# Four of seven low operand parts of the next token block computed ahead and fetched from DRAM; a small Sinkhorn product moved ahead in its slot

## The chip, the cores and the metric

The kernel runs on one core of a Trainium2 chip. The metric is the device time of one execution in microseconds (us); several timed runs are made and their median is given. A profiled execution, which leaves the trace, is made besides.

## The reference

Three stages follow one another, all in float32. Only the second and the third are touched by the change.

```python
def _attn_ref(q, k, v, tau): ...            # thresholded softmax attention, 4 x 8 x 576 x 64

def _moe_ref(x, w1, w2, w3, w_out):         # x: 2304 x 512
    a = x @ w1
    b = x @ w2
    h = a * b @ w3
    return (h @ w_out)

def _moe2_ref(x, w_gate, w1, w2):           # 8 experts
    logits = x @ w_gate
    P = np.exp(logits - logits.max())
    for _ in range(8):
        P /= P.sum(1, keepdims=True) + 1e-09
        P /= P.sum(0, keepdims=True) + 1e-09
        P *= N / E
    out = np.zeros((N, D))
    for e in range(E):
        h = np.maximum(x @ w1[e], 0.0)
        out += P[:, e:e + 1] * (h @ w2[e])
    return out
```

## The kernel before

Attention comes first and leaves x, transposed, in SBUF. In the shadow of the attention the product w3 @ w_out is formed, so that the first layer is `(a * b) @ w34`. From then on one class, `Moe`, does both layers in 120 **units**. A unit takes one piece of 256 hidden columns for one **token block** of 768 tokens. Units 0 to 23 are the first layer: three token blocks of eight units, in turn of kind "a" (x @ w1, kept in `ca`) and kind "b" (x @ w2, multiplied by `ca`). Units 24 to 119 are the eight experts, four units each, for each of the three token blocks. "Block 0" below is units 0 to 7, and a block change is unit 7 to 8, 15 to 16 or 23 to 24.

Each unit forms x @ w (512 deep, 2 x 2 halves) with seven products in place of eight, so it needs seven combinations of the four quarters of x and seven of w. `SLOTS` (line 505) lists the seven **slots**: which operand of x, which of w, which of the two PSUM banks px and py, and whether the slot adds to what is in the bank. Every float32 operand is split into a high part rounded to the matmul's format and a low part, the rest; a slot is six TensorE products (w high x high, w high x low, w low x high, for two halves of the depth), all at line 650. The seven operands of x lie in `xh[i]` and `xl[i]` and serve all units of a block, so at a block change they are made anew: three come straight from x, four from the sums `xs[0]` to `xs[3]`. `xsum` (line 631) makes a sum, on GpSimd (POOL) in slot 5 of the last four units of a block. `xsplit` makes one operand: the high part by a ScalarE copy (ACT, line 638) and the low part by a VectorE subtraction (DVE, line 639). An operand can only be overwritten when the last unit of the block before has used it.

The order of every engine's work is the order in which the code is written. For each slot the loop in `run` (line 857) issues the slot's six products (`mm1`), then `pop`, which sends a share of the second products (h @ w34 or h @ w2, line 720) of the unit before, then `evac`, which moves the slot's result out of PSUM with ACT and DVE, then xsplits, a step of the weight preparation of the next unit (`prep1`, on POOL and ACT), and loads and sums. `FIRST_SPLITS_AT` says after which slot each xsplit comes at a change in the first layer: operands of slots 0 and 1 after slots 4 and 6 of the last unit, those of slots 2 to 6 after slots 0 to 4 of the next unit. Names like u2, v, c, c2, hh and hl (lines 674 to 717) are the steps of `evac`; slots 5 and 6 both use py, so slot 6 can only start when DVE has taken slot 5's result.

Weights of the first layer are prepared in block 0 alone. `keep` (line 555) writes them to DRAM from units 0 to 7, and `prep1` (line 580) reads them back in blocks 1 and 2; the copy out of a buffer must land before the buffer is loaded again. All DMAs are issued by SyncE (SP), in order, on one queue.

After the gate products (line 799) of the last token block, in unit 25, the eight Sinkhorn rounds run as a generator, `sinkhorn`, one small step per slot in units 25 to 30. Each round has one TensorE product of a matrix of ones with the column sums (line 833), which goes to spare columns of px or py; DVE reads the result at line 834.

Of the kernel before, what the change touches and what calls it, by code (L numbers as in the profile page):

```python
# [9 lines left out]
F32 = mybir.dt.float32  # L10
F32R = mybir.dt.float32r
AF = mybir.ActivationFunctionType
ALU = mybir.AluOpType
# [12 lines left out]
HT = SB // 2  # L26
# [2 lines left out]

SPLITS_AT = ((0, 0), (1, 1), (2, 2), (3, 3), (8, 4), (9, 5), (10, 6))  # L30

FIRST_SPLITS_AT = ((4, 0), (6, 1), (7, 2), (8, 3), (9, 4), (10, 5), (11, 6))

CONVERT = (0, 0, 1, 1, 1, 2, 0, 1, 3, 2, 0, 1, 1, 1, 2, 2, 1, 1)
PRODUCTS = (1, 0, 0, 0, 4, 1, 1, 0, 4, 1, 0, 0, 2, 4, 2, 3, 3, 4)
# [28 lines left out]
def f32(ap):  # L64
    return ap.bitcast(F32)
# [434 lines left out]
class Moe:  # L500
# [126 lines left out]
    def xsum(self, s, i, eng):  # L627
# [2 lines left out]
                      (b(0, 1), self.xs[1], ALU.subtract), (b(0, 0), b(1, 0), ALU.subtract))[i]  # L630
        eng.tensor_tensor(out=self.xs[i], in0=x0, in1=x1, op=op)

    def xsplit(self, s, slot):

        i = self.SLOTS[slot][0]
        src = {0: lambda: self.xblock(s, 0, 0), 1: lambda: self.xblock(s, 0, 1), 2: lambda: self.xblock(s, 1, 1),
               3: lambda: self.xs[0], 4: lambda: self.xs[1], 5: lambda: self.xs[3], 6: lambda: self.xs[2]}[i]()
        self.nc.scalar.activation(self.xh[i], src, AF.Copy)  # L638
        self.nc.vector.tensor_tensor(out=self.xl[i], in0=src, in1=f32(self.xh[i]), op=ALU.subtract)  # L639

# [201 lines left out]
    def run(self):  # L842
        units = self.units
        self.raw1[0] = self.k.raw0
        prep = self.prep1(0)
        for slot in range(7):
            if slot < 4:
                self.xsum(0, slot, self.nc.vector)
            self.xsplit(0, slot)
            if slot >= 1:  # L850
                next(prep, None)
            yield
        for _ in prep:
            pass
        sink = None
        gates = {8 * s + (12 if s + 1 < NSB else 9): s for s in range(NSB)}
        for u, (kind, s, j) in enumerate(units):
            nxt = units[u + 1] if u + 1 < len(units) else None
            while u == 1 and self.pool2 is None:
                yield  # L860
            if kind != "a":
                self.hs[u] = tuple(self.pool2.tile([128, 2, SB], F32R, tag=t, name=f"{t}{u}", bufs=2)
                                   for t in ("hh", "hl"))
            ahead = [units[min(u + i, len(units) - 1)][1] for i in range(5)]
            splits = {}
            if ahead[1] != s:
                splits = dict(FIRST_SPLITS_AT if kind == "b" else SPLITS_AT)
            elif u and units[u - 1][1] != s:
                splits = {at - 7: slot for at, slot in (FIRST_SPLITS_AT if units[u - 1][0] == "b" else SPLITS_AT)}
            prep = self.prep1(u + 1)  # L870
            self.load1(u + 2)
            for slot in range(7):
                yield
                late, self.late = self.late[:2], self.late[2:]
                self.mm1(u, slot)
                gate = self.gate(gates[u], slot) if u in gates and slot in (2, 4, 6) else None
                self.pop(slot)
                if sink:
                    try:
                        sink.send(self.xy[1 if slot < 4 else 0])  # L880
                    except StopIteration:
                        sink = None
                self.evac(u, slot)
                if gate:
                    gate()
                    if u == 8 * NSB + 1 and slot == 6:
                        sink = self.sinkhorn()
                        next(sink)
                for f in late:
                    f()  # L890
                if slot in splits:
                    self.xsplit(ahead[1], splits[slot])
                next(prep, None)
                if u < 8 and slot in (1, 2):
                    self.keep(u, slot - 1)
                if slot == 5 and ahead[4] != s:
                    self.xsum(ahead[4], next(i for i in range(4) if ahead[3 - i] == s), self.nc.gpsimd)
                if slot in (3, 5):
                    self.prep2(u + 1 if kind == "a" else u, (slot - 3) // 2)
            while self.later:  # L900
                self.later.pop(0)()
            if kind == "b":
                self.queue_b(u)
                self.left = (2 if nxt[0] == "a" else 1) * (6 + SHARE)
            elif kind != "a":
                self.queue_d(u)
                self.left = 6 + SHARE
        self.left = 0
        self.pop(6)
        for f in self.late:  # L910
            f()
# [3 lines left out]
def kernel(ctx, tc, qk, vv, tau, w1, w2, w3, wo, wg, e1, e2, out):  # L915
    k = Ctx()
# [9 lines left out]
    k.w64 = {"a": w1, "b": w2}  # L926
    k.w34 = dram.tile([4, 128, 2, DM], F32, name="w34")
    k.wab = {n: dram.tile([4, 128, 1024], F32, name=f"w_{n}") for n in ("a", "b")}
    k.wk = dram.tile([8, 2, 128, 7 * 256], F32, name="w_kept")
    k.moe = None  # L930
    attention(k)
# [43 lines left out]
```

## Time and profile before

| | |
|---|---|
| timed runs | 2241.58, 2244.11, 2244.15 us; median 2244.11 |
| profiled execution | 2245.75 us; span of its instructions 2243.8 us |
| granted TensorE clock, mean | 0.996 |
| busy, share of the span | TensorE 97%, VectorE 54%, ScalarE 42%, GpSimd 45% |

The span is the time from the first to the last instruction of the profiled execution; the execution takes 1.95 us more. PE is TensorE, DVE VectorE, ACT ScalarE, POOL GpSimd and SP SyncE. A matmul's shown time overlaps that of its neighbours: two neighbouring 384-column products start 0.17 us apart though each is shown with 0.33 us. An arrow in brackets behind a row gives the idle time of the engine before the instruction and what ended it.

### The profile page before, as it was taken

Reading aid. Unit: us, or ns where it says so; the run is one execution under the profiler, and the core shown is the slowest. Engines: PE = TensorE matmul, PEld = TensorE weight load, DVE = VectorE, ACT = ScalarE, POOL = GpSimd, SP = SyncE. Lnnn points to the kernel's source line nnn. Section 1 sums busy time; section 2 is a strip of 40 time slices with the busy share of each in tenths; the row PEclk is TensorE's granted clock in tenths of the full one; section 3 lists DMA queues with packets and bytes.
Section 4 is the critical chain, followed back from the end, with each engine's and each line's share of the span. In section 5 each row is a group of like instructions: output and inputs, shape, how many; then the busy total and the mean of one; then the engine's idle time right before and its main releaser. Section 6 shows DMA issues by size and latency. Waiting matters only on the chain.

```text
span 2243.8 us, 32239 instructions
## 1 busy us (share of the span) xinstructions
PE 2177.2 (97%) x12624; PEld 1895.7 (84%) x12624; DVE 1222.2 (54%) x2110; ACT 938.4 (42%) x1758; POOL 1013.6 (45%) x982
## 2 busy tenths in 40 slices
PE   7899999899999999999999999999999999999999
PEld 4666666698988888999999999999999999999997
DVE  6888888655455565444445544444445534444443
ACT  6877777532132333333334333333334343333332
POOL 4545444671012444444446544444446444444441
PEclk9999999999999999999999999999999999999999
DMA  4343434455443112122121221212212222121121
GB/s 136 101 129 117 124 107 128 153 205 220 151 182 114 57 57 76 57 76 72 60 75 57 104 75 57 76 58 75 76 57 76 88 72 75 57 76 64 69 75 38
DMA packets 59352, 208.67 MB, mean 93 GB/s; under 512 B 7104, under 2 KB 11200, under 8 KB 59200
## 3 DMA queue, kind: packets, MB, share of 16 engines
q1 hardware_dynamic: 59200, 206.61, 26.6%
q8 instruction: 99, 1.62, 0.3%
q14 instruction: 53, 0.43, 0.1%
HBM read 180.90 MB, written 25.69 MB: 92 GB/s over the span
## 4 chain that ended last, share of the span: by engine, by line
PE 70%; DVE 1%; issue 0%; ACT 0%; POOL 0%; DVEq 0%; ACTq 0%
PE ye L720 36%; PE py L650 19%; PE px L650 14%; DVE xl L639 0%; PE py L799 0%; DVE c L694 0%; PE px L799 0%; DVE c L705 0%; DVE prob L837 0%; ACT xh L638 0%; DVE acc L774 0%; POOL w1l L594 0%; DVE hl L716 0%; POOL w1l L591 0%; DVE small L834 0%
## 5 line engine op out<-in xcount | busy, mean ns | idle before, releaser
L720 PE MATMUL ye<-w2h,hl 128*128 128x512 f32 x1152 | 451.3, 392 | 0.0
L720 PE MATMUL ye<-w2h,hh 128*128 128x512 f32 x1152 | 451.1, 392 | 0.0
L720 PE MATMUL ye<-w2l,hh 128*128 128x512 f32 x1152 | 450.8, 391 | 0.0
L715 ACT ACTIVATE hh<-c 128x384 fp32r<-128x384 f32 x288 | 151.5, 526 | 610.4 <-DVE c L694 610.3
L596 POOL TENSOR_TENSOR w1l<-wt,w1h 128x1024 fp32r<-128x1024 f32 x104 | 252.6, 2429 | 286.2 <-ACT w1h L593 286.2
L650 PE MATMUL py<-xh,w1h 128*128 128x384 f32 x960 | 323.3, 337 | 7.6 <-DVE c L694 3.6
L650 PE MATMUL py<-xl,w1h 128*128 128x384 f32 x960 | 323.1, 337 | 3.5 <-DVE xl L639 3.5
L650 PE MATMUL py<-xh,w1l 128*128 128x384 f32 x960 | 322.7, 336 | 0.3 <-POOL w1l L596 0.3
L591 POOL TENSOR_TENSOR w1l<-raw,w1h 128x256 fp32r<-128x256 f32 x104 | 79.2, 762 | 479.5 <-ACT w1h L585 479.5
L650 PE MATMUL px<-xh,w1h 128*128 128x384 f32 x720 | 243.4, 338 | 4.7 <-ACT p L674 1.6
L650 PE MATMUL px<-xl,w1h 128*128 128x384 f32 x720 | 242.7, 337 | 2.7 <-DVE xl L639 2.7
L720 PEld LDWEIGHTS ye<-w2l,hh 128*128 128x128 f32 x1152 | 216.3, 188 | 32.6
L720 PEld LDWEIGHTS ye<-w2h,hl 128*128 128x128 f32 x1152 | 216.2, 188 | 32.6
L650 PE MATMUL px<-xh,w1l 128*128 128x384 f32 x720 | 242.1, 336 | 0.0
L720 PEld LDWEIGHTS ye<-w2h,hh 128*128 128x128 f32 x1152 | 216.3, 188 | 24.6
L650 PEld LDWEIGHTS py<-xh,w1h 128*128 128x128 f32 x960 | 180.6, 188 | 31.2 <-DVE c L694 6.0
L650 PEld LDWEIGHTS py<-xl,w1h 128*128 128x128 f32 x960 | 180.5, 188 | 22.3 <-DVE xl L639 5.3
L677 DVE TENSOR_TENSOR u<-py,p 128x384 f32<-128x384 f32 x120 | 66.7, 556 | 215.8 <-PE py L650 214.9
L650 PEld LDWEIGHTS py<-xh,w1l 128*128 128x128 f32 x960 | 180.4, 188 | 0.7 <-POOL w1l L596 0.7
L584 POOL TENSOR_TENSOR wt<-raw 128x512 f32<-128x512 f32 x104 | 139.7, 1343 | 77.8 <-DMA raw<-in_e 61.0
L716 DVE SCALAR_TENSOR_TENSOR hl<-c,hh 128x384 fp32r<-128x384 f32 x288 | 165.2, 573 | 9.2
L715 ACT ACTIVATE hh<-px 128x384 fp32r<-128x384 f32 x96 | 47.2, 492 | 272.9 <-PE px L650 272.9
(135 smaller groups left out, 3907.5 us busy)
## 6 DMA issues: line engine op xcount, KB each, us to landing
raw<-in_e SPq DMA_DIRECT2D x192, 512.0 KB, 4.0
wraw<-in_w SPq DMA_DIRECT2D x32, 512.0 KB, 4.1
w1h<-w_kept SPq DMA_DIRECT2D x16, 896.0 KB, 5.2
w1l<-w_kept SPq DMA_DIRECT2D x16, 896.0 KB, 7.0
rq<-in_qk SPq DMA_DIRECT2D x30, 288.0 KB, 5.3
w_kept<-w1h SPq DMA_DIRECT2D x8, 896.0 KB, 7.5
w_kept<-w1l SPq DMA_DIRECT2D x8, 896.0 KB, 9.1
raw<-w SPq DMA_DIRECT2D x12, 512.0 KB, 3.7
```

Of the source, the lines that this page charges most:

```text
L584: nc.gpsimd.tensor_tensor(out=t[:, 0:2], in0=raw[:, 1:3], in1=raw[:, 0:2], op=ALU.subtract)
L591: nc.gpsimd.tensor_tensor(out=wl[:, 0], in0=raw[:, 0], in1=f32(wh[:, 0]), op=ALU.subtract)
L596: nc.gpsimd.tensor_tensor(out=wl[:, 3:7], in0=t, in1=f32(wh[:, 3:7]), op=ALU.subtract)
L650: self.nc.tensor.matmul(out, lhsT=w[:, wi, o], rhs=x[xi][:, d], start=n == 0 and not adds, stop=n == 5, skip_group_check=True)
L677: tt(out=self.u2, in0=py, in1=self.p1, op=ALU.add)
L715: nc.scalar.activation(hi, src, AF.Relu)
L716: self.later.append(lambda: nc.vector.scalar_tensor_tensor(out=lo, in0=src, scalar=0.0, in1=f32(hi), op0=ALU.max, op1=ALU.subtract))
L720: self.queue.append((out.shape[-1], lambda: self.nc.tensor.matmul(out, lhsT=l, rhs=r, start=start, stop=stop, skip_group_check=True)))
```

## The change

Four things change.

1. For the operands of slots 0 to 3 at each of the three block changes of the first layer, the low parts are computed ahead. `xstage` makes the high part (ACT) and the low part (DVE) in the still unused accumulator `acc`, and SP stores the low part in a DRAM tensor `x_low`. It runs after slot 3 of the block's unit 2, slots 1 and 5 of unit 4 and slot 2 of unit 6 (`STAGED`).
2. At the change, `xturn` replaces `xsplit` for these four: ACT writes the high part again and SP loads the low part, after slots 1 to 4 of the block's last unit, one slot after the operand's last use. The other three operands are split as before, after slots 1 to 3 of the next unit.
3. The sums `xs` for these three changes are made on DVE, after slots 0 and 5 of unit 2 and slots 0 and 3 of unit 4 (`XSUMS`), instead of on POOL. The copies of unit 7's weights to DRAM go from slots 1 and 2 to slots 4 and 5.
4. The Sinkhorn step of a slot is issued before `pop` instead of behind it, and its ones product goes to px after slots 2, 4 and 5 and to py after the others (before: py up to slot 3, px from slot 4 on).

The block changes of the second layer keep their order.

```diff
-FIRST_SPLITS_AT = ((4, 0), (6, 1), (7, 2), (8, 3), (9, 4), (10, 5), (11, 6))
+XSUMS = {2: (0, 5), 4: (0, 3)}
+STAGED = {2: ((3, 0),), 4: ((1, 1), (5, 2)), 6: ((2, 3),)}
+NEXT_SB = (1, 2, 0)
...
+    def xstage(self, r, slot, n):
+
+        src = self.xsource(NEXT_SB[r], self.SLOTS[slot][0])
+        flat = self.acc.rearrange("p a b -> p (a b)")
+        hi, lo = (flat[:, 2 * HT * (2 * n + m):2 * HT * (2 * n + m + 1)].bitcast(F32R) for m in range(2))
+        split = lambda t: t.rearrange("p (a b) -> p a b", a=2)
+        self.nc.scalar.activation(split(hi), src, AF.Copy)
+        self.nc.vector.tensor_tensor(out=split(lo), in0=src, in1=split(f32(hi)), op=ALU.subtract)
+        self.nc.sync.dma_start(self.k.xk[r, slot], f32(lo))
+
+    def xturn(self, r, slot):
+
+        i = self.SLOTS[slot][0]
+        self.nc.scalar.activation(self.xh[i], self.xsource(NEXT_SB[r], i), AF.Copy)
+        self.nc.sync.dma_start(f32(self.xl[i]).rearrange("p a b -> p (a b)"), self.k.xk[r, slot])
...
-            splits = {}
-            if ahead[1] != s:
-                splits = dict(FIRST_SPLITS_AT if kind == "b" else SPLITS_AT)
+            splits, turns = {}, {}
+            if kind == "b" and ahead[1] != s:
+                turns = {i + 1: i for i in range(4)}
+            elif u and units[u - 1][0] == "b" and units[u - 1][1] != s:
+                splits = {i - 3: i for i in range(4, 7)}
+            elif ahead[1] != s:
+                splits = dict(SPLITS_AT)
             elif u and units[u - 1][1] != s:
-                splits = {at - 7: slot for at, slot in (FIRST_SPLITS_AT if units[u - 1][0] == "b" else SPLITS_AT)}
+                splits = {at - 7: slot for at, slot in SPLITS_AT}
...
-                self.pop(slot)
                 if sink:
                     try:
-                        sink.send(self.xy[1 if slot < 4 else 0])
+                        sink.send(self.xy[0 if slot in (2, 4, 5) else 1])
                     except StopIteration:
                         sink = None
+                self.pop(slot)
                 self.evac(u, slot)
...
-                if u < 8 and slot in (1, 2):
-                    self.keep(u, slot - 1)
-                if slot == 5 and ahead[4] != s:
+                at = 4 if u == 7 else 1
+                if u < 8 and slot in (at, at + 1):
+                    self.keep(u, slot - at)
+                if slot in turns:
+                    self.xturn(u // 8 if kind == "b" else u // 8 - 1, turns[slot])
+                if kind in ("a", "b"):
+                    if slot in XSUMS.get(u % 8, ()):
+                        self.xsum(NEXT_SB[u // 8], u % 8 - 2 + XSUMS[u % 8].index(slot), self.nc.vector)
+                    for at, x in STAGED.get(u % 8, ()):
+                        if slot == at:
+                            self.xstage(u // 8, x, at // 3 % 2)
+                elif slot == 5 and ahead[4] != s:
                     self.xsum(ahead[4], next(i for i in range(4) if ahead[3 - i] == s), self.nc.gpsimd)
...
+    k.xk = dram.tile([3, 7, 128, 2 * HT], F32, name="x_low")
```

The order of the instructions shows where this moves work. First DVE at the first block change, from the last results of unit 7 to slot 6 of unit 8. In the names the number behind u2, v, c, c2, hh and hl is the unit (and the next one the slot), the number behind xl and xh the operand, and the last number only tells tiles apart. Before:

```order
L694 TENSOR_TENSOR c_7_4_6038<-px_5189,v_7_3_6027 128x384
L639 TENSOR_TENSOR xl0_5117<-x_63,xh0_5110 128x768
L694 TENSOR_TENSOR c_7_5_6053<-py_5190,v_7_3_6027 128x384
...
L639 TENSOR_TENSOR xl4_5121<-s1_5125,xh4_5114 128x768
L705 TENSOR_TENSOR c2_7_6_6069<-c_7_6_6067,ca_5228 128x384
...
L639 TENSOR_TENSOR xl1_5118<-x_63,xh1_5111 128x768
L677 TENSOR_TENSOR u2_8_1_6109<-py_5190,p1_8_0_6090 128x384
L639 TENSOR_TENSOR xl3_5120<-s0_5124,xh3_5113 128x768
L639 TENSOR_TENSOR xl6_5123<-s2_5126,xh6_5116 128x768
L680 TENSOR_TENSOR v_8_3_6138<-py_5190,u2_8_1_6109 128x384
L639 TENSOR_TENSOR xl5_5122<-s3_5127,xh5_5115 128x768
```

The changed kernel, the same place:

```order
L726 TENSOR_TENSOR c2_7_6_6088<-c_7_6_6086,ca_5229 128x384
L728 TENSOR_TENSOR hl7_5995<-c2_7_5_6074,hh7_5994 128x384
L728 TENSOR_TENSOR hl7_5995<-c2_7_6_6088,hh7_5994 128x384
L698 TENSOR_TENSOR u2_8_1_6124<-py_5191,p1_8_0_6107 128x384
L660 TENSOR_TENSOR xl6_5124<-s2_5127,xh6_5117 128x768
L660 TENSOR_TENSOR xl5_5123<-s3_5128,xh5_5116 128x768
L701 TENSOR_TENSOR v_8_3_6153<-py_5191,u2_8_1_6124 128x384
L660 TENSOR_TENSOR xl2_5120<-x_63,xh2_5113 128x768
```

Four of the seven subtractions into xl are gone from here; xl6, xl5 and xl2 now stand nearer to the start of unit 8.

Second, SP's queue from the same unit 7 on, in the changed kernel (w_kept are the weights kept in DRAM, raw2 the weights of the second products; the number behind w1h and w1l is the unit):

```order
L608 DMA raw2_11_5983<-w34_64 128x1024
L582 DMA w1h8_6006<-w_kept_68 128x1792
L582 DMA w1l8_6007<-w_kept_68 128x1792
L653 DMA xl0_5118<-x_low_67 128x768
L653 DMA xl4_5122<-x_low_67 128x768
L653 DMA xl1_5119<-x_low_67 128x768
L557 DMA w_kept_68<-w1h7_5900 128x1792
L653 DMA xl3_5121<-x_low_67 128x768
L557 DMA w_kept_68<-w1l7_5901 128x1792
L582 DMA w1h9_6109<-w_kept_68 128x1792
L582 DMA w1l9_6110<-w_kept_68 128x1792
```

Before, the same rows stood there in the same order without the four loads of xl. The loads are new, and each waits for the slot that last used its buffer.

Third, DVE in unit 2 of the changed kernel, from the end of unit 1's work to the end of unit 2's (ca is where an a unit's results go):

```order
L728 TENSOR_TENSOR hl1_5361<-c2_1_6_5446,hh1_5360 128x384
L633 TENSOR_TENSOR s0_5125<-x_63 128x768
L698 TENSOR_TENSOR u2_2_1_5486<-py_5191,p1_2_0_5467 128x384
L701 TENSOR_TENSOR v_2_3_5517<-py_5191,u2_2_1_5486 128x384
L646 TENSOR_TENSOR acc_5341<-x_63,acc_5341 128x768
L711 TENSOR_TENSOR ca_5229<-px_5190,v_2_3_5517 128x384
L711 TENSOR_TENSOR ca_5229<-py_5191,v_2_3_5517 128x384
L633 TENSOR_TENSOR s1_5126<-s0_5125,x_63 128x768
L621 TENSOR_TENSOR w2l3_5552<-raw2_3_5344,w2h3_5524 128x1024
L711 TENSOR_TENSOR ca_5229<-py_5191,u2_2_1_5486 128x384
```

The rows at lines 633 (two sums) and 646 (the staged low part) are new here; the rest stands as before.

## Rows read from the trace of the kernel before

**Rows 1.** The page: busy time of the engines; a group of POOL's weight preparation.
```profile
PE 2177.2 (97%) x12624; PEld 1895.7 (84%) x12624; DVE 1222.2 (54%) x2110; ACT 938.4 (42%) x1758; POOL 1013.6 (45%) x982
...
L584 POOL TENSOR_TENSOR wt<-raw 128x512 f32<-128x512 f32 x104 | 139.7, 1343 | 77.8 <-DMA raw<-in_e 61.0
```

**Rows 2.** PE's timeline (start us, duration us, instruction): first products of units, two waits.
```profile
469.20 0.44 PE L650 MATMUL px<-xh,w1h 128*128 128x384 f32 x1 [0.15 <-ACT p L674]
...
493.85 0.44 PE L650 MATMUL px<-xh,w1h 128*128 128x384 f32 x1 [1.44 <-ACT p L674]
...
502.69 0.34 PE L650 MATMUL px<-xh,w1h 128*128 128x384 f32 x1
...
513.65 0.34 PE L650 MATMUL px<-xh,w1h 128*128 128x384 f32 x1
...
531.22 0.33 PE L650 MATMUL px<-xh,w1h 128*128 128x384 f32 x1
...
542.17 0.34 PE L650 MATMUL px<-xh,w1h 128*128 128x384 f32 x1
...
554.16 0.34 PE L650 MATMUL px<-xh,w1h 128*128 128x384 f32 x1
...
761.03 0.33 PE L650 MATMUL px<-xh,w1h 128*128 128x384 f32 x1
...
846.08 0.34 PE L650 MATMUL px<-xh,w1h 128*128 128x384 f32 x1
...
861.63 0.34 PE L650 MATMUL px<-xh,w1h 128*128 128x384 f32 x1
```

**Rows 3.** Busy us: PE, PEld, DVE, ACT, POOL; clock, DMA share, GB/s; PE's longest wait.
```profile
515.00:531.00 16.00, 12.32 (x67) 10.20 (x67) 13.35 (x16) 6.71 (x10) 9.24 (x4) 1.00 0.34 114
716.00:739.00 23.00, 19.43 (x103) 16.51 (x102) 19.35 (x24) 10.62 (x17) 16.50 (x11) 1.00 0.00 1
...
PE py L650 <- DVE xl L639: 1.1, 2, 0.6
```

**Rows 4.** By line: durations ns min/median/max, first and last start us.
```profile
L639 DVE TENSOR_TENSOR xl<-s,xh x24: 921/959/2125, 411.7 to 1739.3; 128x768 fp32r<-128x768 f32 x24
...
L638 ACT ACTIVATE xh<-s x24: 827/836/849, 410.8 to 1738.4; 128x768 fp32r<-128x768 f32 x24
```

**Rows 5.** Timelines of DVE and of POOL around 487 us, in unit 5.
```profile
486.76 0.56 DVE L694 TENSOR_TENSOR c<-py,v 128x384 f32<-128x384 f32 x1 [0.94 <-PE py L650]
487.23 2.04 DVE L705 TENSOR_TENSOR c<-c,ca 128x384 f32<-128x384 f32 x1
...
484.40 2.65 POOL L596 TENSOR_TENSOR w1l<-wt,w1h 128x1024 fp32r<-128x1024 f32 x1 [2.26 <-ACT w1h L593]
487.01 1.85 POOL L631 TENSOR_TENSOR s<-s,x 128x768 f32<-128x768 f32 x1
```

**Rows 6.** PE's timeline at one of the eight ones products.
```profile
804.24 0.39 PE L720 MATMUL ye<-w2l,hh 128*128 128x512 f32 x1
804.47 0.28 PE L833 MATMUL py<-small,ones 128*128 128x8 f32 x2
805.67 0.44 PE L650 MATMUL px<-xh,w1h 128*128 128x384 f32 x1 [0.92 <-DVE hl L716]
```

**Rows 7.** DMA in 502:517 (packets, MB, share; issue, landing us); SP's timeline; a stretch.
```profile
q1 hardware_dynamic: 795, 4.73, 92.9%
...
w_kept<-w1l SPq DMA_DIRECT2D x1, 896.0 KB, 11.8
...
513.50 0.32 SPq L580 DMA_DIRECT2D w1h<-w_kept  x1
515.78 0.32 SPq L580 DMA_DIRECT2D w1l<-w_kept  x1
...
534.00:536.00 2.00, 2.00 (x12) 1.87 (x11) 1.10 (x2) 0.00 (x0) 0.00 (x0) 1.00 1.06 428
```

**Rows 8.** The stretches' view again, 444:446.
```profile
444.00:446.00 2.00, 1.87 (x8) 1.58 (x8) 1.88 (x4) 1.50 (x4) 0.21 (x1) 0.50 0.83 221
```

More of the change, by code (lines that the diff above doesn't have):

```diff
@@ L631, in xsum, with xsource @@
         eng.tensor_tensor(out=self.xs[i], in0=x0, in1=x1, op=op)
+    def xsource(self, s, i):
+        return {0: lambda: self.xblock(s, 0, 0), 1: lambda: self.xblock(s, 0, 1), 2: lambda: self.xblock(s, 1, 1),
+               3: lambda: self.xs[0], 4: lambda: self.xs[1], 5: lambda: self.xs[3], 6: lambda: self.xs[2]}[i]()
+    def xstage(self, r, slot, n):
[10 more added lines that the diff above has]
+        self.nc.sync.dma_start(f32(self.xl[i]).rearrange("p a b -> p (a b)"), self.k.xk[r, slot])
     def xsplit(self, s, slot):
         i = self.SLOTS[slot][0]
-        src = {0: lambda: self.xblock(s, 0, 0), 1: lambda: self.xblock(s, 0, 1), 2: lambda: self.xblock(s, 1, 1),
-               3: lambda: self.xs[0], 4: lambda: self.xs[1], 5: lambda: self.xs[3], 6: lambda: self.xs[2]}[i]()
+        src = self.xsource(s, i)
         self.nc.scalar.activation(self.xh[i], src, AF.Copy)
```

## The prediction

> **What bounds the kernel now.** I read the page first. TensorE (PE) is busy 97% of the span [rows 1], so time can only come out of the few stretches in which PE stands still or runs slowly; everything on other engines counts only where PE waits for it. Next I read PE's timeline for the start of each unit: 42 L650 products a unit, seven slots of six, always beginning with px<-xh,w1h. The reader should see how even the starts are where nothing waits: 542.17 to 554.16 is 11.99 us for an a unit, 502.69 to 513.65 is 10.96 us for a b unit, 846.08 to 861.63 is 15.55 us for a unit of the second layer [rows 2]. Excess over these lengths is what a stall really costs, more than the idle time shown, because the product after a stall also starts the pipe again.
>
> Four places have excess. (1) Unit 8, the first of token block 1: 513.65 to 531.22 is 17.57 us, 5.58 too long. (2) Unit 16 repeats it a block later, 5.51 too long (its rows read like those of unit 8, the second of two such places). (3) Units 23 and 24: no unit of like length stands beside 24, so I go by idle time: PE is idle 3.57 us in 716:739 against 3.68 in 515:531 [rows 3], and 5.58 x 3.57 / 3.68 = 5.4. (4) Units 26 to 30, the Sinkhorn: 761.03 to 846.08 is 85.05 us, five units of 15.55 are 77.75, so 7.30; eight pairs of ones products at 0.28 [rows 6] are 2.24 of it and stay, 5.06 is waiting. A fifth is small: unit 6 waits 1.44 us at 493.85 [rows 2].
>
> Who is waited for? In 515:531 the longest waits of PE are for DVE's xl split [rows 3]. The split is seven ACT copies (0.84 us) and seven DVE subtractions of 0.96 us that stretch to 2.1 us [rows 4]. Why they stretch is seen best at 487: POOL starts a sum of 1.85 us at 487.01, and DVE's c<-c,ca, which reads only SBUF, takes 2.04 us and ends 0.41 us after POOL, while c<-py,v of the same size, with an operand in PSUM, had run in 0.56 us under another POOL instruction [rows 5]. I read this as exclusion: a DVE instruction that reads only SBUF and one of POOL wait for each other whole.
>
> **The change, part by part.**
>
> *Block changes (units 7/8, 15/16, 23/24).* Four of the seven DVE subtractions leave each change and become a DMA; three stay, one in each of slots 1 to 3 of the next unit. Working through unit 8 from its start at 513.65 with slots of 1.63 us (1.04 and five short L720 products): DVE loses xl0, xl4, xl1 and xl3 (4 x 0.96) ahead of u2 and v, POOL's sums no longer run beside it, and the other three, each behind its ACT copy (0.84), end about 4.6, 6.8 and 8.2 us in, while slots 4, 5 and 6 want them 6.7, 8.3 and 10.5 us in. ACT's copies start four slots earlier; the last ends before slot 5. So I take all 16.5 us (5.58 + 5.51 + 5.4) and give back what is late next. That is the DMA queue in unit 7: SP issues raw2, two kept loads, xl0, xl4, xl1, a copy out, xl3, a copy out, then unit 9's loads. The queue is already 92.9% busy in 502:517 [rows 7]; 4 x 384 KB = 1.57 MB add 3.7 us at the 428 GB/s of 534:536 and 4.6 us at the 339 that 4.73 MB in 92.9% of 15 us make. Unit 9's loads were issued at 513.50 and 515.78, when the copies out of the same buffers had landed; now the second goes out about 3.9 us later, at 519.6, landing near 525.5 to 527, while unit 9 would start at 525.6. I take 0.4 us (bounds 0 and 1.4). In units 23 and 24 POOL still prepares weights, so xl5 and xl2 meet it: 0.3 (bounds 0 and 1.5). Unit 16 has no copies out: 0.1. Sum -15.7. If instead every load took the 11.8 us of the slowest row, xl0 (issued at 503.8) would be 1.8 us late and unit 9 about 3 us; 3 us at each of three changes leave -7.5, the worst end.
>
> The Trainium skill ("DMA: Bandwidth & Descriptors", Specifications) puts a core's HBM limit at about 358 GB/s; the 428 of rows 7 lies above it, so the trace disagrees. By the page the four loads would take 4.4 us and unit 9 would wait 1.1 us instead of 0.4, 0.7 us more in all.
>
> *Staging in units 2, 4, 6 and 10 to 22.* Each block gets four sums on DVE (the size of xl, so 0.96 us where POOL is quiet), four ACT copies (0.84) and four subtractions (0.96) [rows 4]. In blocks 1 and 2 POOL has nothing to do, and an a unit leaves DVE over 1 us free in most slots: nothing, except units 12 and 20, where the gate products write py right behind slot 2 and u2, one sum later, is not yet out of it: 0.15 each, 0.3. Block 0 is different: POOL prepares weights in every slot, and the eight added instructions read SBUF only. Unit 2, from the end of slot 5's products: copy out of py 0.56, s1 0.96, w2l 1.2, next copy out 0.56, 3.3 us in all. PE wants the bank again, in unit 3's slot 1, after 3.9 us: eight L720 products of 0.23 [rows 6] and two slots of 1.04 (a b unit is 42 and 16 products: (10.96 - 16 x 0.23) / 7). So 0.6 us are spare, and s1 and w2l, each meeting a POOL weight instruction of up to 1.34 us (L584 [rows 1]) half way through, take 1.4: 0.8 late. Unit 4 has the same chain with a subtraction in the sum's place (0.5, since PE has been held once already) and, before it, s3 behind POOL's longest instruction, 2.65 us [rows 5], of which some 1.7 are left and the slots' slack covers half: 0.9, together 1.4. Against that, POOL's sum at 487.01 goes; what stays is what unit 4 shows at the same place, where POOL has only weights: an idle of 0.15 us at 469.20 against 1.44 at 493.85 [rows 2], 1.3 gained. Block 0 nets +0.9. Bounds: -1.6 (both idles gone, no new wait) and +2.9 (units 2 and 4 each as bad as unit 6 was).
>
> SP's twelve stores and the later raw loads behind them: raw1_7 leaves some 2.5 us later and lands about 1 us before POOL wants it; nothing. The moved copy-out of unit 7 is in the queue sum above.
>
> *Sinkhorn.* The ones product moves ahead of the slot's four to eight L720 products. At 804.47 it is the last of its slot; on DVE hl<-px stands behind the reading of its result, and PE's next slot waits 0.92 us for hl [rows 6]. Sent first, it is done about 1.15 us (five L720 products of 0.23) earlier, more than the 0.92. All eight places have at least four such products, 0.92 us. The bank choice keeps the next slot's bank free in all but one case, which has 1.15 us to spare. New danger: PE now waits if DVE's column sums are not ready at the end of the slot; only in unit 27 are they close. Of 5.06 I take 4.1 (bounds 0 and 5.1).
>
> **Sum.** -15.7 + 0.9 + 0.3 - 4.1 = -18.6 us. The profiled execution took 2245.75 us, which gives 2227.2; it lies 1.64 above the median of the three timed runs (2244.11), so for the median 2225.5. I forecast **2225.5 us**.
>
> **The rivals.** *The wait moves into block 0:* the eight added DVE instructions meet POOL harder than I count, units 2 to 6 each lose what unit 6 lost. For: POOL prepares weights there in every unit. Against: a units have slack. Five units by 1.44 are 7.2 in place of 0.9: 2231.8.
>
> *The low parts land late:* the loads take the slowest row's time, block changes give 7.5 instead of 15.7: 2233.7. For: 92.9% of the queue is taken. Against: only unit 7 has copies out beside them.
>
> *Slower:* the new stalls of units 2 and 3 stand right behind a stretch at a granted clock of 0.50, the 1.2 GHz level (444:446 [rows 8]): 8 matmuls in 2 us, against 12 at full clock in 534:536 [rows 7]. If they bring that level back, a unit of 12 us takes half as long again, 6 us more. From (18.6 + 4.5) / 6 = 3.9 units on, the kernel is slower by over 0.2%; five units give 2225.5 + 30 = 2255.5. Against: 3.68 us of idle in 515:531 left the clock at 1.00 [rows 3]. The Trainium skill ("TensorE: Matmul & The Clock Gate", Part 1) calls the low level the default and says that activity lifts it; by that rule a change that takes idle out of PE can hardly lower it, and no run here shows otherwise.
>
> *The relief does nothing:* ACT, which still makes all seven copies in order, becomes what is waited for; 5 us a change come back, 2242. Against: ACT was busy 6.71 of the 16 us of 515:531 [rows 3].
>
> **How the numbers follow.** Forecast 0.63, block 0 0.13, late loads 0.14, no relief 0.06, slower 0.04. About 0.2% (4.5 us) is the least that a measurement of this kernel tells from no change. The first three are faster: 0.90; no relief counts as the same: 0.06; slower 0.04. Low end: 2244.1 - 16.5 - 1.6 - 5.1 = 2220.9, so 2220.5. High end: late loads with a Sinkhorn that gives 2 less, 2235.7, so 2236.
>
> **What would show it.** Right: units 8 and 16 last under 12.6 us, no PE wait on xl or xh at 515 to 531; unit 9 starts within 0.5 us; units 26 to 30 sum to about 81 us; DVE subtractions in units 2 and 4 of 1.5 to 3 us beside POOL. Wrong: PE waits for an xl DMA in units 8, 16 or 24, units 2 to 5 above 13.5 us, granted clock under 1 after 446 us, or ones products followed by waits as long as now.

## The result and the profile after

| | before | after |
|---|---|---|
| timed runs, us (median; from, to; five each) | 2244.11; 2241.39, 2244.31 | 2220.82; 2218.66, 2223.54 |
| ratio, 95% interval | | 0.9903 [0.9889, 0.9916] |
| span of the profiled execution, us | 2243.8 | 2221.6 |
| from the start of unit 3 to the end of the last matmul, us | 1783.70 | 1763.05 |

The change makes the kernel 1.0% faster. The forecast was 2225.5 us, the range 2220.5 to 2236. The direction was right, and so was the mechanism of the two large terms; the forecast was 4.7 us too cautious, and the result lies just above the low end. The last row of the table is the sharpest measure. Ahead of unit 3 executions of one program differ: unit 3 began at 450.2 to 454.7 us in the thirteen profiles of this study. From unit 31 to the last matmul all thirteen took between 1392.2 and 1392.3 us. So below I compare units with units.

The page of the changed kernel, busy time of the engines, answers to [rows 1]:

```profile
PE 2171.8 (98%) x12624; PEld 1894.7 (85%) x12624; DVE 1229.4 (55%) x2122; ACT 947.1 (43%) x1770; POOL 990.9 (45%) x970
```

PE has the same number of matmuls; twelve instructions are gone from POOL, and DVE and ACT have twelve more each. POOL lost 22.7 us of busy time for twelve sums. DVE gained only 7.2 us, where twelve more instructions of 0.96 us are 11.5 us: some of its busy time before was stretching.

PE's timeline of the changed kernel (start us, duration us, instruction, in brackets the idle before it and what ended it), first products of units 7, 8, 9, 26 and 31, beside [rows 2]:

```profile
502.55 0.34 PE L671 MATMUL px<-xh,w1h 128*128 128x384 f32 x1
...
513.51 0.34 PE L671 MATMUL px<-xh,w1h 128*128 128x384 f32 x1
...
525.49 0.34 PE L671 MATMUL px<-xh,w1h 128*128 128x384 f32 x1
...
744.64 0.33 PE L671 MATMUL px<-xh,w1h 128*128 128x384 f32 x1
...
825.47 0.34 PE L671 MATMUL px<-xh,w1h 128*128 128x384 f32 x1
```

Unit 8 lasts 11.98 us, what an a unit takes with no wait, instead of 17.57. Units 26 to 30 last 80.83 in place of 85.05. The stretches (busy us and count of PE, PEld, DVE, ACT, POOL; clock, DMA share, GB/s) around units 8 and 24, where [rows 3] had 3.68 and 3.57 us of PE idle:

```profile
508.00:524.00 16.00, 16.00 (x97) 15.26 (x96) 10.89 (x19) 7.71 (x12) 0.00 (x0) 1.00 0.97 345
...
708.00:724.00 16.00, 16.00 (x94) 14.96 (x93) 14.35 (x20) 8.23 (x14) 11.50 (x9) 1.00 0.01 2
```

In these two stretches PE does not stand still at all. All waits of PE from 504 to 828 us (engine, line, released by: us in total, times, longest):

```profile
PE px L854 <- DVE small L851: 0.4, 1, 0.4
```

One is left, the ones product of unit 27, which the forecast named as the new danger. It costs more than the 0.4 us shown: unit 27 lasts 17.24 us, 1.2 more than units 29 and 30, which have as many ones products and last 16.00 and 16.02. By line, DVE's subtractions: the three that stayed at the block change (500 to 530 us), and the staged ones from x in units 2 and 4 (durations in ns, min/median/max):

```profile
L660 DVE TENSOR_TENSOR xl<-s,xh x2: 959/959/959, 517.0 to 519.3; 128x768 fp32r<-128x768 f32 x2
L660 DVE TENSOR_TENSOR xl<-x,xh x1: 950/950/950, 520.6 to 520.6; 128x768 fp32r<-128x768 f32 x1
...
L646 DVE TENSOR_TENSOR acc<-x,acc x2: 2089/2324/2559, 449.4 to 476.2; 128x768 fp32r<-128x768 f32 x2
```

Against [rows 4]: the stretched subtractions are gone from the block change and stand in block 0 instead, 2.6 us in unit 2 and 2.1 us in unit 4, beside POOL's weight work. Only the one in unit 4 costs PE anything that a run shows (block 0 at slot 6, below).

### The profile page after: what moved, and what is told of

Read it like the earlier page. It is cut to its first block, busy times and chain, and to the rows that moved or that the text cites. A ratio compares the mean times of both kernels' runs of the same rounds, so it can differ in the third digit from the quotient of the medians.

```text
span 2221.6 us, 32300 instructions
## 1 busy us (share of the span) xinstructions
PE 2171.8 (98%) x12624; PEld 1894.7 (85%) x12624; DVE 1229.4 (55%) x2122; ACT 947.1 (43%) x1770; POOL 990.9 (45%) x970
## 4 chain that ended last, share of the span: by engine, by line
PE 92%; DVE 6%; issue 1%; ACT 1%; DMA 1%; POOL 0%; SPq 0%; ACTq 0%; DVEq 0%; POOLq 0%
PE ye L741 40%; PE py L671 22%; PE px L671 16%; PE s L142 4%; PE pv L232 3%; PE t L186 2%; PE w L460 2%; DVE p L161 2%; DVE nmx L146 2%; PE vs L209 1%; PE tt L197 1%; PE py L820 0%; DVE x L281 0%; DVE cvq L495 0%; DVE c L726 0%
## 5 line engine op out<-in xcount | busy, mean ns | idle before, releaser
L741 PE MATMUL ye<-w2h,hl 128*128 128x512 f32 x1152 | 451.6, 392 | 0.0
L741 PE MATMUL ye<-w2h,hh 128*128 128x512 f32 x1152 | 451.3, 392 | 0.0
L741 PE MATMUL ye<-w2l,hh 128*128 128x512 f32 x1152 | 451.0, 391 | 0.0
L741 PEld LDWEIGHTS ye<-w2l,hh 128*128 128x128 f32 x1152 | 216.3, 188 | 32.9 <-DVE w2l L621 0.3
L741 PEld LDWEIGHTS ye<-w2h,hl 128*128 128x128 f32 x1152 | 216.2, 188 | 32.6
L741 PEld LDWEIGHTS ye<-w2h,hh 128*128 128x128 f32 x1152 | 216.3, 188 | 24.6
```

The costliest lines, as they stand in the source:

```text
L741: self.queue.append((out.shape[-1], lambda: self.nc.tensor.matmul(out, lhsT=l, rhs=r, start=start, stop=stop, skip_group_check=True)))
```

## The experiments

Two theories stood behind the forecast's largest term: DVE's queue of seven in-order subtractions, and POOL's sums that shut DVE out. The experiments take them apart, put a price on the DMA queue and on the Sinkhorn's two edits, and look at what the forecast had missed. Lengths of units in us, one profile each (the two profiles of before and of the change in one column where they agree within 0.05):

| | before | change | sums only | staging only | ones late | copies early | loads beside |
|---|---|---|---|---|---|---|---|
| unit 5 | 10.96 | 11.96, 11.36 | 10.96 | 11.50 | 11.96 | 11.36 | 11.36 |
| unit 6 | 13.72 | 12.43 | 12.41 | 13.70 | 12.43 | 12.40 | 12.41 |
| unit 7 | 10.96 | 10.96 | 10.96 | 12.79 | 10.96 | 10.97 | 10.96 |
| unit 8 | 17.57 | 11.98 | 15.08 | 13.52 | 11.98 | 14.69 | 15.57 |
| unit 16 | 17.50 | 11.98 | 15.06 | 12.00 | 11.98 | 11.97 | 11.98 |
| units 23, 24 | 32.01 | 26.62 | 31.55 | 27.41 | 26.62 | 26.62 | 26.62 |
| units 26 to 30 | 85.05 | 80.83, 81.10 | 81.24 | 80.88 | 85.38 | 81.20 | 80.73 |

**Sums only.** Nothing is staged, the sums stay on DVE:

```diff
-STAGED = {2: ((3, 0),), 4: ((1, 1), (5, 2)), 6: ((2, 3),)}
+STAGED = {}
+FIRST_SPLITS_AT = ((4, 0), (6, 1), (7, 2), (8, 3), (9, 4), (10, 5), (11, 6))
...
-                turns = {i + 1: i for i in range(4)}
+                splits = dict(FIRST_SPLITS_AT)
...
-                splits = {i - 3: i for i in range(4, 7)}
+                splits = {at - 7: slot for at, slot in FIRST_SPLITS_AT}
```

> The sums stay on VectorE and ahead, but nothing is staged: all seven subtractions go back to the block change, in the slots they had. My theory (VectorE's own queue of in-order subtractions in front of PE's u2 and v copies is the larger part of the loss, POOL's sums beside them the smaller): unit 8 and unit 16 last 14 to 15.5 us, each with about 3 us of PE waits, unit 5 falls from 11.96 to about 11.0 because its staged pair is gone; time 2228 to 2230 us. Rival (POOL's sums, which lock VectorE out, are the whole cause, and moving the sums alone would have done): units 8 and 16 last 12.0 to 12.5 us, time 2220 to 2222 us.

2231.7 us, ratio to before 0.9947 [0.9932, 0.9962]. By line, DVE's subtractions of this kernel from 500 to 530 us, and PE's waits from 508 to 524:

```profile
L661 DVE TENSOR_TENSOR xl<-s,xh x4: 949/954/959, 511.0 to 518.9; 128x768 fp32r<-128x768 f32 x4
L661 DVE TENSOR_TENSOR xl<-x,xh x3: 948/951/959, 505.7 to 520.3; 128x768 fp32r<-128x768 f32 x3
```
```profile
PE px L672 <- DVE xl L661: 0.5, 1, 0.5
PE py L672 <- DVE xl L661: 0.5, 1, 0.5
PE px L672 <- ACT xh L660: 0.4, 1, 0.4
PE py L672 <- ACT xh L660: 0.3, 1, 0.3
```

With POOL idle no subtraction is stretched any more, and yet unit 8 keeps 3.10 of its 5.59 us. So the queue of splits alone costs 3.1 us, and POOL's sums beside it had added 2.5. At the third change, where POOL has weights to prepare anyway, taking its sums away gives only 0.5 of 5.4 us. I had named units 8 and 16 alone, and the time came out 1.7 us above the top of what I expected. Part of the 3.10 is ACT: its copies, in the old places, are late too (0.7 us of the 1.7 us of waits), so the change's earlier copies matter beside the staged low parts. No run moved the copies alone, so how the 3.10 divide between copies and subtractions is not shown.

**Staging only.** The staging stays, the sums go back to POOL. Since POOL makes the sum for slot 1's operand only in unit 5, that operand's staging moves from unit 4 to slot 5 of unit 6:

```diff
-XSUMS = {2: (0, 5), 4: (0, 3)}
-STAGED = {2: ((3, 0),), 4: ((1, 1), (5, 2)), 6: ((2, 3),)}
+STAGED = {2: ((3, 0),), 4: ((5, 2),), 6: ((2, 3), (5, 1))}
...
-                    if slot in XSUMS.get(u % 8, ()):
-                        self.xsum(NEXT_SB[u // 8], u % 8 - 2 + XSUMS[u % 8].index(slot), self.nc.vector)
+                    if slot == 5 and u % 8 > 3:
+                        self.xsum(NEXT_SB[u // 8], u % 8 - 4, self.nc.gpsimd)
```

> The other half alone: four low parts are staged as in the change, but the sums go back to POOL in slot 5 of units 4 to 7 of each block. Theory (three subtractions are few enough, and POOL's last sum is over before they begin): units 8 and 16 last 12.0 to 12.5 us; unit 6 gets its wait back, 13.4 to 13.8 us against 12.43, unit 5 loses its own, 11.0 to 11.4; time 2220.5 to 2223 us. Rival (the sums must leave POOL, staging is not enough): units 8 and 16 last 13.5 us or more, time 2225 us or above.

2224.35 us, ratio 0.9914 [0.9899, 0.9929]. In unit 16 the theory holds to 0.02 us, though a sum of POOL's still stretches one of its three subtractions to 1.85 us: three have room for it, seven had not. So the staging, with its earlier copies, is what that block change needed, and POOL's sums cost there only while the long queue stood. At the third change 0.8 us of 5.4 are lost. In block 0 the theory does not hold: units 7 and 8 lose 1.83 and 1.54 us, and the time is 1.35 us above the top of what I expected. DVE's, then POOL's timeline of this kernel at the end of unit 6, and PE's first product behind them:

```profile
498.84 1.82 DVE L645 TENSOR_TENSOR acc<-s,acc 128x768 fp32r<-128x768 f32 x1
500.59 2.87 DVE L620 TENSOR_TENSOR w2l<-raw,w2h 128x1024 fp32r<-128x1024 f32 x1
503.38 0.55 DVE L710 TENSOR_TENSOR ca<-py,u 128x384 f32<-128x384 f32 x1
```
```profile
497.99 1.86 POOL L632 TENSOR_TENSOR s<-x,s 128x768 f32<-128x768 f32 x1
499.80 2.57 POOL L632 TENSOR_TENSOR s<-x 128x768 f32<-128x768 f32 x1
```
```profile
504.07 0.41 PE L670 MATMUL py<-xh,w1h 128*128 128x384 f32 x1 [1.59 <-DVE ca L710]
```

Two DVE instructions with both operands in SBUF run in turn with two of POOL's and take 4.6 us where they need 2.2; the copy out of py stands behind them. The next load of raw waits for the second of them, w2l, and goes out at 503.52, 2.7 us after the start of unit 7 and not 0.7 before it; the low parts' loads stand behind it, and unit 8 waits 1.3 us for one. The first of the two is the staging that this experiment itself had moved to unit 6. So in block 0 the sums could not stay on POOL with the staging laid out like this; whether another layout would do was not tried. At the change into block 2 they need not have left.

**Copies early.** The copies out of unit 7's weights go back ahead of the loads:

```diff
-                at = 4 if u == 7 else 1
+                at = 1
```

> Only the copies out of unit 7's weights move back to slots 1 and 2, ahead of the loads of xl4, xl1 and xl3 in SP's queue. Theory (the loads share one DMA queue with them, and xl3 has under 1 us to spare in unit 8, landing at 517.74 us where PE wants it at about 518.5): 0.9 MB more ahead of xl3 at 428 GB/s are 2.1 us, unit 8 lasts 12.5 to 13.8 us and PE waits for the xl DMA; unit 9's second load lands no later than now. Units 16 and 24 as now, time 2221.5 to 2223 us. Rival (the sixteen DMA engines serve all transfers in flight at once, so the order of issue hardly matters): unit 8 stays within 0.2 us of 11.98.

2223.3 us, ratio 0.9910 [0.9894, 0.9927]. Right in direction, short in size: unit 8 loses 2.71 us. PE's timeline:

```profile
511.08 0.45 PE L671 MATMUL px<-xl,w1h 128*128 128x384 f32 x1 [0.95 <-DMA xl<-x_low]
...
514.21 0.44 PE L671 MATMUL py<-xl,w1h 128*128 128x384 f32 x1 [1.21 <-DMA xl<-x_low]
```

I had looked at the wrong operand. SP sends one copy ahead of xl0 and both ahead of xl4, and PE waits for these two, in slots 0 and 1; xl3, the one I had named, was not waited for. The two waits add up to 2.16 us, and each has a restart behind it. The line that moves these copies by three slots, which looks like housekeeping in the diff, carries 2.7 us.

**Loads twice.** Each load of a low part is sent twice to the same buffer:

```diff
-        self.nc.sync.dma_start(f32(self.xl[i]).rearrange("p a b -> p (a b)"), self.k.xk[r, slot])
+        for _ in range(2):
+            self.nc.sync.dma_start(f32(self.xl[i]).rearrange("p a b -> p (a b)"), self.k.xk[r, slot])
```

> Each of the four loads of low parts is sent twice, 1.57 MB more in the queue of each block change, the arithmetic unchanged. Theory (after unit 7's copies the queue has little room: unit 9's second load now lands 1.05 us before PE wants it, xl3 some 0.8 us before): the extra loads take 3.7 to 4.6 us of the queue, so units 8 and 9 together lose 2.6 to 5 us, while at the other two changes, without copies out, units 16, 17, 24 and 25 lose under 0.5 us together; time 2223.5 to 2226 us. Rival (loads are cheap in this queue: the transfers in flight overlap and the engines have room): units 8 and 9 lose under 0.5 us, time as the change.

2251.34 us, ratio 1.0039 [1.0024, 1.0054]: far above both the theory and the rival. Unit 8 lasts 25.67 us, unit 16 21.93. The second load writes what the first writes, so SP waits for the first to land before it sends the second, and all that stands behind it in SP's queue waits too. In SP's timeline (start, time over which the group is issued) the first three pairs take 15.65 us to issue, against 3.32 for the three single loads of the change:

```profile
503.38 15.65 SPq L654 DMA_DIRECT2D xl<-x_low  x6
```

That measured a wait in SP's queue, not the queue's room. So:

**Loads beside.** The second load goes into the staging buffer, which then has no other use:

```diff
+        self.nc.sync.dma_start(self.acc.rearrange("p a b -> p (a b)")[:, 2 * HT * slot:2 * HT * (slot + 1)], self.k.xk[r, slot])
```

> As the kernel that loaded each low part twice, but the second load goes to the staging buffer, which nothing uses then, so it waits for no earlier landing: 1.57 MB more in the queue of each block change, without a wait in SP's queue. Theory (in unit 7 the engines have no room left): the extra 3.7 to 4.6 us of transfers less unit 9's margin of 1.05 us come back as PE waits, units 8 and 9 together lose 2 to 4 us, the other two changes under 1 us each; time 2222.5 to 2226 us. Rival (what the doubled loads cost was all the wait of each second load for the landing of the first): units 8 and 9 lose under 0.5 us.

2224.15 us, ratio 0.9915 [0.9901, 0.9929]; unit 8 loses 3.59 us, units 16 and 24 nothing. Transfers land in the order of issue: the first two loads and their doubles landed at 505.89, 506.86, 507.87 and 508.81, one every 0.97 us, 405 GB/s for the 0.39 MB of each. At that pace the four extra loads take 3.9 us, inside the forecast's 3.7 to 4.6; the third pair was slower, 1.25 and 1.57 us behind what landed before. But PE stood still for 1.78 us only. PE's timeline, and the stretches behind it:

```profile
515.55 0.45 PE L672 MATMUL py<-xl,w1h 128*128 128x384 f32 x1 [1.78 <-DMA xl<-x_low]
```
```profile
513.00:517.00 4.00, 2.22 (x15) 1.96 (x14) 1.24 (x3) 2.90 (x4) 0.00 (x0) 0.95 1.04 422
517.00:520.00 3.00, 3.00 (x13) 3.00 (x13) 1.47 (x3) 0.00 (x0) 0.00 (x0) 0.50 0.86 315
520.00:523.00 3.00, 3.00 (x18) 2.75 (x17) 1.59 (x4) 0.00 (x0) 0.00 (x0) 1.00 0.74 294
```

The other half is the clock: a granted 0.50, the 1.2 GHz level, from 517 to 520, behind one idle of 1.78 us. I had expected all of the loss as waits for the queue; that its size came out inside the 2 to 4 us expected is in part luck.

**Ones late.** The Sinkhorn's order and its choice of banks are undone:

```diff
+                self.pop(slot)
...
-                        sink.send(self.xy[0 if slot in (2, 4, 5) else 1])
+                        sink.send(self.xy[1 if slot < 4 else 0])
...
-                self.pop(slot)
```

> Only the Sinkhorn's order is undone: the ones product is again sent behind the slot's short products, with the old choice of bank. Theory: units 26 to 30 go back from 80.8 to about 85.0 us, 4.2 us more, all of it PE idle in front of px products that wait for VectorE's hl; block changes unchanged; time 2225 us. Rival (part of what units 26 to 30 gained comes from their start being moved against the weight loads by the 16 us gained before): they lose less than 3 us, time under 2224 us.

2223.25 us, ratio 0.9912 [0.9897, 0.9927]; units 26 to 30 last 85.38 us, 4.55 more than in the first profile of the change and 4.28 more than in its second. The median came out below the 2225 us expected; by the units the loss is all there, and the lowest timed run, 2222.90, is 4.2 us above the lowest of the change. Not all of it is in front of px products that wait for hl, as I had expected (1.5 us): the largest wait from 750 to 835 us is that of py products for DVE's c.

```profile
PE py L671 <- DVE c L715: 1.8, 2, 0.9
```

The same product, of the fourth round, in PE's timeline of this kernel and in that of the change:

```profile
786.70 0.28 PE L854 MATMUL py<-small,ones 128*128 128x8 f32 x2
787.90 0.44 PE L671 MATMUL px<-xh,w1h 128*128 128x384 f32 x1 [0.92 <-DVE hl L737]
```
```profile
785.27 0.28 PE L854 MATMUL py<-small,ones 128*128 128x8 f32 x2
...
786.65 0.34 PE L671 MATMUL px<-xh,w1h 128*128 128x384 f32 x1
```

The wait of 0.92 us, the same as in [rows 6], is gone when the product precedes its slot's five L741 products.

**Old banks.** The product is first in its slot, but in the bank it had before:

```diff
-                        sink.send(self.xy[0 if slot in (2, 4, 5) else 1])
+                        sink.send(self.xy[1 if slot < 4 else 0])
```

> The ones product stays first in its slot, but takes the bank it took before the change (one bank up to slot 3, the other from slot 4). Theory (the product's place in the slot gives the gain, the choice of bank only keeps it from waiting for a bank that a VectorE copy still reads): units 26 to 30 last 80.8 to 83 us, that is, 0 to 2.2 us of the 4.2 are lost; time 2221 to 2223 us. Rival (the bank is what counts): they go back to about 85 us; time 2225 us.

2220.01 us, ratio 0.9905 [0.9889, 0.9922]; units 26 to 30 81.63. Only unit 27 is longer, 18.01 us against 17.14 to 17.62 in the other profiles that send the product first. There the product waits for its bank, until DVE has read u out of py; PE's only wait from 740 to 825 us:

```profile
PE py L854 <- DVE u L698: 0.9, 1, 0.9
```

The place in the slot makes the gain; the bank is worth 0.4 to 0.9 us, by one profile, and the timed runs do not show it.

**Staging at slot 6.** The second staging of units 4, 12 and 20 moves a slot on, to get unit 5's new wait back:

```diff
-STAGED = {2: ((3, 0),), 4: ((1, 1), (5, 2)), 6: ((2, 3),)}
+STAGED = {2: ((3, 0),), 4: ((1, 1), (6, 2)), 6: ((2, 3),)}
```

> The second staging of unit 4 (12, 20) moves from slot 5 to slot 6. Theory (unit 5's 1.0 us is VectorE's ca copy standing behind the staged subtraction and w2l in the last slots of unit 4): unit 5 falls from 11.96 to 10.96 to 11.2 us, nothing else moves; time 2219.8 to 2222 us, about 1 us less than the change in its units. Rival (the subtraction only moves its delay one slot on): units 5 and 6 together last as long as now, 24.2 to 24.5 us.

2222.18 us, ratio 0.9912 [0.9897, 0.9926]. Unit 5 falls to 10.97 as expected, but unit 22 rises from 11.98 to 13.17. SP's, POOL's, DVE's and PE's timelines of this kernel show a chain through four engines:

```profile
673.55 0.32 SPq L647 DMA_DIRECT2D x_low<-acc  x1
...
674.91 0.46 SPq L568 DMA_DIRECT2D raw<-in_e  x1
```
```profile
683.45 1.41 POOL L586 TENSOR_TENSOR wt<-raw 128x512 f32<-128x512 f32 x1 [185.88 <-DMA raw<-in_e]
```
```profile
683.62 1.65 DVE L728 TENSOR_TENSOR hl<-c,hh 128x384 fp32r<-128x384 f32 x1
```
```profile
687.27 0.44 PE L671 MATMUL px<-xh,w1h 128*128 128x384 f32 x1 [0.90 <-ACT p L695]
```

In unit 21 the store of the low part, now a slot later, holds the load of the first expert's weights behind it in SP's queue. The load lands 0.4 us after the start of unit 22 in place of 3.0 before it, POOL starts on it, and DVE's hl, 0.55 us when alone, meets POOL and takes 1.65. What stands behind hl on DVE comes late, and with it ACT's p, for which PE waits.

**Block 0 at slot 6.** The same in unit 4 alone, not in units 12 and 20:

```diff
-                        if slot == at:
+                        if slot == at + (u == 4 and at == 5):
```

> The second staging of unit 4 moves to slot 6 in token block 0 alone; in units 12 and 20 it stays in slot 5. Theory (unit 5's 1.0 us comes from that staging; unit 22's 1.2 us in the kernel that moved all three came from the store that SP sends ahead of the next weights' load in unit 21, which put POOL's work beside VectorE's hl): unit 5 lasts 10.96 us, unit 22 11.98 us, everything else as in the change, so 1.0 us less in the units; the median moves by less than a measurement tells, 2218 to 2222 us. Rival (the two effects are chance of the run): unit 5 or unit 22 is long again.

Units 5 and 22 last 10.96 and 11.98 us, so both causes named above hold. From unit 3 to the last matmul it takes 1762.19 us, 0.9 and 0.6 less than the two profiles of the change; the timed median, 2220.59 us, ratio 0.9905 [0.9891, 0.9919], does not tell it from the change.

**Before again** and **after again.** Both kernels, unedited:

> The kernel before, profiled once more. Theory (the 1.54 us by which its last store took longer after the last matmul, 5.47 us against 3.93, and the start of unit 3 at 454.66 us belong to that execution and not to the kernel): the tail is 3.9 to 4.4 us here and unit 3 starts somewhere from 450 to 455 us, while units 3 to 30 last as in the first profile within 0.3 us together, except unit 5 or 6. Rival (the change shortens the tail): 5.3 to 5.6 us again.

> The changed kernel, profiled once more. Theory: units 6 to 30 as in the first profile within 0.3 us together, the stretch ahead of unit 3 different by up to 4 us, the tail 3.9 to 4.4 us; unit 5's wait of 1.0 us depends on where POOL's weight instructions fall and lies between 0 and 1.1 us. Rival (the gains read from one profile are that profile's): units 8, 16, 24 or the Sinkhorn's differ by over 0.5 us.

Timed: 2243.49 us (ratio to before 1.0001 [0.9992, 1.0010]) and 2221.54 (0.9903 [0.9889, 0.9917]). The units repeat: unit 8 17.59 and 11.98, unit 16 17.52 and 11.98, from unit 3 to the last matmul 1783.69 and 1762.77. Unit 5 of the change is 11.36 this time. But my theory of the end of the program falls: after the last matmul the kernel before takes 5.48 us again, the change 3.94 again. The DMA view of the end, of before again (2238.9 to 2243) and of the change (2218.5 to 2222): queues, and issues with KB and us to landing:

```profile
q1 hardware_dynamic: 333, 0.58, 38.3%
q14 instruction: 1, 0.01, 0.5%
...
out<-acc SPq DMA_DIRECT2D x1, 256.0 KB, 3.1
```
```profile
q1 hardware_dynamic: 341, 0.60, 45.7%
...
out<-acc SPq DMA_DIRECT2D x1, 256.0 KB, 2.0
```

Before, one packet of the instruction queue falls beside the last store, which takes 3.1 us in place of 2.0. Of the other kernels only two have such a packet there: loads twice, whose last store took 2.57 us, and loads beside, 2.12. In all the rest there is none and the store takes 2.0. That such a packet delays the store agrees with all thirteen profiles, but the delay runs from 0.1 to 1.1 us, and no run put a packet there on purpose: the cause is argued, not shown. The rest of the 1.54 us (0.4) lies between that store's landing and the end of the program.

## Why the prediction was right, and where it was short

- **Block changes, -15.7 forecast, -16.5 measured** (units 8, 16, 23 and 24: -5.59, -5.52, -0.99, -4.38). The mechanism and place were right. What I gave back did not come. Unit 9 was to start 0.4 us late; its second load was issued at 520.34, 0.7 us later than forecast, but landed in 4.45 us, 1.05 us ahead of need, because only one load was left in the queue ahead of it. The queue's price itself was about right, 3.9 us at the pace of loads beside. The 0.3 for units 23 and 24 and the 0.1 for unit 16 did not show. The margin was thin all the same, as copies early shows. The DMA view of the change in 502:517 and SP's timeline, against [rows 7]:

```profile
q1 hardware_dynamic: 1189, 5.13, 95.2%
...
xl<-x_low SPq DMA_DIRECT2D x4, 384.0 KB, 7.4
```
```profile
516.84 0.32 SPq L582 DMA_DIRECT2D w1h<-w_kept  x1
520.34 0.32 SPq L582 DMA_DIRECT2D w1l<-w_kept  x1
```

- **The split of that gain** was left open in the forecast: both causes were named and removed together. Sums only leaves 3.1 of unit 8's 5.6 us, so moving the sums is worth 2.5 there; staging only takes all of unit 16's 5.5. At these two the queue is the cause, and POOL's sums made it longer. At the third change staging only leaves 0.8 of 5.4 us, and sums only 4.9.
- **Block 0, +0.9 forecast, -0.1 and -0.8 measured** (units 3 to 7 together, first and second profile). Unit 6 gave its 1.3 as foreseen. Unit 5 paid 1.0, in the second profile 0.4, of the 1.4. The step that failed is the stretching in unit 2: s1 and w2l were to lose 1.4 us to POOL, and with 0.6 spare to hold PE up by 0.8. They took 1.12 and 1.76 us, 0.7 more than the 2.16 they need, and PE was 0.14 late. In unit 4 the 0.9 for s3 did not come either: s3 started just ahead of POOL's longest instruction and took 1.00 us. All of unit 5's 1.0 is the staged subtraction (2.09 us), for which I had taken 0.5 with w2l behind it: block 0 at slot 6 gets it all back. So the two sizes there were wrong in opposite directions. How long two engines hold each other up depends on where their instructions fall, and I had taken half of an instruction of POOL's or more each time. DVE's timeline of the change in units 2 and 4:

```profile
452.79 1.12 DVE L633 TENSOR_TENSOR s<-s,x 128x768 f32<-128x768 f32 x1
453.83 1.76 DVE L621 TENSOR_TENSOR w2l<-raw,w2h 128x1024 fp32r<-128x1024 f32 x1
...
472.81 1.00 DVE L633 TENSOR_TENSOR s<-x 128x768 f32<-128x768 f32 x1
...
476.19 2.09 DVE L646 TENSOR_TENSOR acc<-x,acc 128x768 fp32r<-128x768 f32 x1
```

- **Gates in units 12 and 20, +0.3**: +0.33.
- **Sinkhorn, -4.1**: -4.2 and -4.0. Ones late confirms it. The parts were less exact than the sum: a pair of ones products costs 0.23 us (unit 28, 15.78 against 15.55), not 0.28, so there were 5.5 us of waiting and not 5.06, and 1.2 of them are left in unit 27. I had also read only the wait for hl; the wait for c is as long.
- **Missed: the end of the program, -1.5.** No step of the forecast looked behind the last matmul. Without it the median would have come out near 2222.4 us.
- **The sum** in the profile is -22.2 for -18.6: 0.8 from the block changes, 1.0 from block 0, 1.5 from the end, 0.2 from the Sinkhorn and unit 25. The remaining 1.1 of 4.7 us is how the two profiled executions stand to their medians.
- **The rivals.** The waits did not move into block 0. The rival of no relief was put at 2242 us; at the 5 us a change given there it would be 2240.5. That the low parts land late did not come true in the change, only in runs that moved or added loads or copies (copies early, staging only, loads beside). That ACT would be waited for is refuted: the change has no wait for xh, though sums only, with the copies late, shows 0.7 us of it. The clock stayed at 1.00 in both stretches above. My argument against it, though, that 3.68 us of idle had left the clock alone, was weaker than I took it for: that idle came in pieces of at most 0.8 us, the longest this wait of before from 515 to 531 us, and in loads beside the low level came right behind one piece of 1.78 us.

```profile
PE py L650 <- DVE ca L690: 0.8, 1, 0.8
```

## What to carry to other kernels

When in-order work queues up in front of a product, shorten the queue first: a neighbour's lock that had cost 2.5 us beside seven subtractions (unit 8) cost nothing beside three (unit 16 of staging only). Work moved ahead is paid for in DMA order: in a single issuing queue a store one slot later cost 1.2 us a unit away, and copies three slots earlier cost 2.7 us. Move a small product whose result is read by a busy engine to the front of its slot.

## What the runs showed of the hardware

- A granted clock of 0.50 for 3 us, the level of [rows 8], followed one PE idle of 1.78 us (loads beside), and the late transfer cost twice its wait, 3.59 us. The length of the idle alone does not tell when this happens: an idle of 1.59 us in staging only left the clock at 1.00, and so did two of 2.1 us in loads twice, while in that same kernel four stretches of 0.50 lie within or behind idles of 1.9 to 5.2 us. PE's timeline of loads twice, and the stretch that holds both idles:

```profile
635.16 0.44 PE L672 MATMUL px<-xl,w1h 128*128 128x384 f32 x1 [2.13 <-DMA xl<-x_low]
...
639.18 0.45 PE L672 MATMUL py<-xl,w1h 128*128 128x384 f32 x1 [2.12 <-DMA xl<-x_low]
```
```profile
630.60:640.00 9.40, 4.62 (x27) 4.11 (x28) 2.38 (x3) 2.90 (x4) 0.00 (x0) 1.00 0.66 228
```

- DVE instructions that read only SBUF and instructions of POOL exclude each other in these rows too, not only where I first read it [rows 5]: 1.82 and 2.87 us in place of 0.95 and 1.2 in staging only, 1.65 in place of 0.55 in unit 22 of staging at slot 6. The Trainium skill ("SBUF — State Buffer", SBUF: two separate sides) calls the shared ports an exclusive lock held for a whole instruction; these rows agree.
- Transfers on the one queue landed in the order of issue, in all thirteen profiles. A low part of 0.39 MB landed 0.97 us behind the one before it where loads followed loads, against 7.3 to 10.5 us from its issue to its landing (loads beside), so nearly all of that time is waiting for what was issued before.
- Where a packet of the instruction queue fell beside the last store, the store took longer: by 1.1 us in both profiles of before, by 0.5 and 0.1 in two other kernels. The kernels differ only up to unit 30, some 1390 us before that store.
